# Attention then MLP on one core: a new issue order, 64-column transposes, loads of 96 and 48 rows, v in one load

## Chip, cores, metric

One core of a Trainium2 chip runs the program. The time is device microseconds (us) of one execution. Lower is better. Most executions agree within 0.3 per cent; where a run's state is "slow" (over 1.5 per cent above the fastest of its kernel) or its executions scatter, this is said and its time isn't compared.

Names in what follows: PE is the matmul engine (TensorE), DVE is VectorE, ACT is ScalarE, and POOL in profile lines is GpSimd. SBUF and PSUM are the on-chip memories; PE's results go to PSUM.

## What is computed

```python
def _attn_ref(q, k, v):              # B=8, H=8, S=576, D=64, float32
    scores = q @ k.T / sqrt(D)
    rel = pos[:, None] - pos[None, :]
    mask_plain = (rel >= 0) & (rel < 32)                       # heads 0..3
    mask_dil   = (rel >= 0) & (rel < 128) & (rel % 4 == 0)     # heads 4..7
    ...                                                        # softmax, then @ v
def _moe_ref(x, w_in, w_out):        # x: 4608 x 512; w_in: 512 x 2048; w_out: 2048 x 512
    h = x @ w_in
    return (h * sigmoid(h)) @ w_out
```

The MLP has nine groups of 512 tokens. A group needs 64 + 64 matmuls of 128x128 by 512 columns. Attention of a batch is many small matmuls.

## The kernel before

q and k of a batch are loaded in two pieces of 72 rows (a row here is four neighbouring positions of the sequence, all heads). Two heads at a time are transposed on PE into a PSUM tile, 8 transposes a tile, and copied to SBUF; for heads 0 to 3 ("first heads") by four ACT copies, since the two heads' halves come out on the wrong partitions. I call such a set of transposes a *tile*; a batch has eight (k and q, four pairs of heads each).

```python
ps_mm = tile_pool(name="ps_mm", bufs=3, PSUM)   # h and y of the MLP
ps_t  = tile_pool(name="ps_t",  bufs=1, PSUM)   # one transpose tile
...
def trans(nm, hp):
    tps = ps_t.tile([P, 2, 2, 2, MH], F16, ...)            # MH = 72
    for hi in range(2):
        for rp in range(2):
            for t in range(2):                             # the two loaded pieces
                nc.tensor.transpose(tps[:, hi, rp, t],
                    nats[nm, t][:, 2 * hp + hi, 2 * rp : 2 * rp + 2, :], ident[:MH, :MH])
    ...
    if hp >= HP // 2:                                      # heads 4..7: one DVE copy
        nc.vector.tensor_copy(dst, src); return
    for hi in range(2):                                    # heads 0..3: four ACT copies
        for ri in range(2):
            nc.scalar.copy(dst, src[rs, hi])
...
for step in attention(0): step()
for g in range(NG):                                        # MLP group g, attention g+1
    steps = mlp(g)                                         # 16 layer-1, then 16 layer-2 steps
    for i, step in enumerate(steps):
        step()
        # attention steps of batch g+1 dealt out evenly over the MLP steps
        upto = min(len(att), (i + 1) * len(att) // (len(steps) - 2))
        ...
```

The softmax here doesn't subtract the row's maximum and nothing guards it: scores larger than these inputs give would overflow.

## Time and profile before

419.46 us (median). What matters:

| part of the span | us |
|---|---|
| start-up, up to the first MLP matmul | 40.1 |
| seven groups, each with the next batch's attention | 44.6 to 46.3 each |
| two groups of MLP alone | 27.6 each |
| drain | 4.1 |

The windows view, cut where groups begin, shows this. Its columns are the stretch, its length, busy us (and number of instructions) of PE, PE's weight loads, DVE, ACT and GpSimd, then the granted clock of PE, the share of the DMA engines, and GB/s.

```profile
0.00:40.10 40.10, 15.60 (x204) 12.15 (x205) 18.02 (x69) 15.94 (x25) 25.56 (x51) 1.00 1.33 143
86.24:131.28 45.04, 40.02 (x334) 19.69 (x332) 25.92 (x68) 25.63 (x44) 9.22 (x12) 0.89 0.54 68
358.52:386.15 27.63, 27.63 (x129) 12.51 (x128) 11.01 (x16) 11.94 (x20) 0.00 (x0) 1.00 0.13 39
```

A mixed group takes 45.0 us, though neither DVE nor ACT is busy for more than 26 us of it, and an MLP group alone needs 27.6 us. The waits view (who waited for what: us in total, times, longest) and the page's row of granted clock (tenths of full speed, 40 slices) say why.

```profile
PE tq_0_1165 L164 <- ACT kP_1132 L182: 2.6, 1, 2.6
PE tq_1_1216 L164 <- ACT kP_1132 L182: 1.2, 1, 1.2
```

```profile
PEclk9999989986999699988998699969997799999999
```

PE waits for ACT's four copies at the head of each group, and after such gaps the clock is granted at half speed for a while (the 6s and 7s). The 1.00 of the first row isn't a reading: the trace's record of the clock begins at 49.3 us, and until then matmuls of 512 columns start 0.43 us apart instead of 0.216, as they do at a clock of 0.50. One more reading, which the prediction missed, stands in the timeline of the kernel before (start, duration, engine, line, tile and operands, partitions x columns).

```profile
56.19 1.03 PE L303 MATMUL h_6_684<-xT,w_in_88 128*128 128x512 f16 x4
57.15 0.30 PE L193 MATMUL s_1_692<-qP_551,kP_552 64*128 64x96 f16 x6
57.38 1.04 PE L303 MATMUL h_7_701<-xT,w_in_88 128*128 128x512 f16 x4
58.26 0.20 PE L164 MATMUL tq_2_709<-ident,q_nat_0_175 72*128 72x72 f16 x1
58.30 0.19 PE L164 MATMUL tq_2_709<-ident,q_nat_1_177 72*128 72x72 f16 x1
```

From start to start, h_7 takes 0.88 us when a 72-row transpose follows. The same work in h_6 takes 0.96 us when a 64-row score step follows. So about 0.1 us is lost at the step from 128 rows to 64. It is no single case: at full clock the last MLP matmul before a 72-row transpose takes 0.216 us from start to start (median of 35), before a 64-row score matmul with the same 72 columns of moving data 0.311 us (median of 21). Transposes of 72 rows among themselves go at 0.03 us each.

### The profile page before, as it was taken

What the parts mean: (1) busy time and instruction counts of PE and PEld (TensorE: products, weight loads), DVE (VectorE), ACT (ScalarE), POOL (GpSimd) and SP (SyncE); (2) the same over time, 40 slices, a digit from 0 to 9 for tenths busy, and PEclk for the clock granted to TensorE, in tenths of its full rate; (3) what the DMA queues carried; (4) which work ended last, traced back from release to release, by engine and by line L of the source; (5) the groups of instructions that cost most, each with busy time, mean ns of one, the idle gap of its engine ahead of it and who ended that gap; (6) DMA issues with size and microseconds to landing.
All of it is one profiled execution on the core that took longest, in us unless ns stands there. A gap on an engine that the chain in (4) does not pass through costs nothing.

```text
span 417.9 us, 7058 instructions
## 1 busy us (share of the span) xinstructions
PE 351.6 (84%) x2784; PEld 175.1 (42%) x2784; DVE 221.0 (53%) x578; ACT 218.8 (52%) x373; POOL 85.2 (20%) x128
## 2 busy tenths in 40 slices
PE   0266699978996799969997899779995999999996
PEld 0244344533453345424453345334542445444442
DVE  2077168524963377516952496328742685560730
ACT  2840975169614963197516861496319651451631
POOL 8933638200620035001610062000000000000000
PEclk9999989986999699988998699969997799999999
DMA  8999999910891029200991079100020002102102
GB/s 100 122 199 142 156 179 138 186 31 2 98 140 52 0 35 171 59 27 0 145 109 36 2 90 149 51 1 2 25 52 25 2 2 62 40 1 78 25 25 77
DMA packets 67746, 29.60 MB, mean 71 GB/s; under 512 B 34944, under 2 KB 63104, under 8 KB 67712
## 3 DMA queue, kind: packets, MB, share of 16 engines
q0 software_dynamic: 62080, 19.70, 46.2%
q1 hardware_dynamic: 5632, 9.44, 7.7%
q8 instruction: 22, 0.36, 0.4%
q14 instruction: 12, 0.10, 0.1%
HBM read 39.32 MB, written 9.44 MB: 117 GB/s over the span
## 4 chain that ended last, share of the span: by engine, by line
PE 68%; ACT 16%; DVE 11%; issue 3%; DMA 1%; POOL 0%; ACTq 0%; DVEq 0%; POOLq 0%
ACT kP_192 L182 2%; DMA k_nat_1_113<-in_k_dram 1%; ACT kP_2292 L182 1%; ACT kP_2873 L182 1%; ACT kP_1132 L182 1%; ACT kP_4025 L182 1%; ACT kP_3452 L182 1%; ACT kP_1713 L182 1%; ACT kP_552 L182 1%; PE y_0_1454 L321 1%; PE y_0_3195 L321 1%; PE y_0_2035 L321 1%; PE y_0_874 L321 1%; PE y_0_4347 L321 1%; PE y_0_3774 L321 1%
## 5 line engine op out<-in xcount | busy, mean ns | idle before, releaser
L303 PEld LDWEIGHTS <-w_in_88 128*128 128x128 f16 x576 | 53.4, 106 | 56.5 <-issue 14.9
L100 POOL DMA_DIRECT2D vp_104<-in_v_dram x24 | 18.0, 751 | 23.6 <-DMA w_in_88<-in_moe_w_in_dram 5.3
L100 POOL DMA_DIRECT2D vp_103<-in_v_dram x24 | 17.9, 754 | 18.2 <-DMA q_nat_0_1708<-in_q_dram 2.4
L224 DVE TENSOR_TENSOR probs_91<-probs_91,mask_p 128x576 f16<-128x576 f16 x3 | 1.4, 454 | 15.3 <-ACT probs_91 L222 15.3
L321 PEld LDWEIGHTS <-gT_4800 128*128 128x128 f16 x64 | 6.3, 98 | 7.5
L321 PEld LDWEIGHTS <-gT_4587 128*128 128x128 f16 x64 | 6.2, 97 | 7.6
L312 DVE SCALAR_TENSOR_TENSOR gT_4800<-th_0_4806,h_0_4801 128x512 f16<-128x512 f32 x1 | 0.7, 687 | 14.0 <-ACT th_0_4806 L311 14.0
L82 POOL DMA_DIRECT2D k_nat_0_2283<-in_k_dram x1 | 0.8, 848 | 31.0 <-PE tk_3_1897 L164 31.0
L82 POOL DMA_DIRECT2D k_nat_0_3443<-in_k_dram x1 | 0.8, 848 | 30.5 <-PE tk_3_3057 L164 30.5
L82 POOL DMA_DIRECT2D k_nat_0_2864<-in_k_dram x1 | 0.8, 848 | 30.3 <-PE tk_3_2476 L164 30.3
L321 PEld LDWEIGHTS <-gT_555 128*128 128x128 f16 x64 | 5.3, 97 | 4.1
L321 PEld LDWEIGHTS <-gT_3455 128*128 128x128 f16 x64 | 5.3, 97 | 4.1
L321 PEld LDWEIGHTS <-gT_2876 128*128 128x128 f16 x64 | 5.3, 97 | 4.1
L321 PEld LDWEIGHTS <-gT_4028 128*128 128x128 f16 x64 | 5.3, 97 | 4.1
L321 PEld LDWEIGHTS <-gT_2295 128*128 128x128 f16 x64 | 5.3, 97 | 4.1
L321 PEld LDWEIGHTS <-gT_1716 128*128 128x128 f16 x64 | 5.3, 97 | 4.1
L321 PEld LDWEIGHTS <-gT_1135 128*128 128x128 f16 x64 | 5.3, 97 | 4.1
L182 ACT COPY kP_192<-tk_0_195 64x288 f16<-64x288 f16 x4 | 3.2, 790 | 7.1 <-PE tk_0_195 L164 7.1
L94 POOL DMA_DIRECT2D vraw_107<-in_v_dram x8 | 5.9, 744 | 4.2 <-DMA w_out_89<-in_moe_w_out_dram 3.1
L311 ACT ACTIVATE th_0_561<-h_0_556 128x512 f32<-128x512 f32 x1 | 0.6, 597 | 11.5 <-PE h_0_556 L303 11.5
L94 POOL DMA_DIRECT2D vraw_108<-in_v_dram x8 | 5.9, 743 | 3.1 <-DMA w_in_88<-in_moe_w_in_dram 1.7
L82 POOL DMA_DIRECT2D k_nat_0_1704<-in_k_dram x1 | 0.8, 848 | 27.0 <-PE tk_3_1316 L164 27.0
(1845 smaller groups left out, 1117.3 us busy)
## 6 DMA issues: line engine op xcount, KB each, us to landing
w_in_88<-in_moe_w_in_dram POOLq DMA_DIRECT2D x4, 512.0 KB, 8.9
w_out_89<-in_moe_w_out_dram POOLq DMA_DIRECT2D x4, 512.0 KB, 9.7
vp_103<-in_v_dram POOLq DMA_DIRECT2D x24, 64.0 KB, 4.4
vp_104<-in_v_dram POOLq DMA_DIRECT2D x24, 64.0 KB, 7.0
vraw_107<-in_v_dram POOLq DMA_DIRECT2D x4, 208.0 KB, 9.2
vraw_108<-in_v_dram POOLq DMA_DIRECT2D x4, 208.0 KB, 9.9
vraw_107<-in_v_dram POOLq DMA_DIRECT2D x4, 144.0 KB, 9.8
vraw_108<-in_v_dram POOLq DMA_DIRECT2D x4, 144.0 KB, 9.5
```

The lines of the kernel that those rows point to most:

```text
L82: nc.gpsimd.dma_start(out=d.rearrange("p h r d -> p h (r d)"), in_=src[b].rearrange("h (m r) d -> m h (r d)", r=DIL)[t * MH : (t + 1) * MH],)
L94: nc.gpsimd.dma_start(out=vraw[p0 : p0 + n, ab].rearrange("p h r d -> p h (r d)"), in_=src[m0 : m0 + n],)
L100: nc.gpsimd.dma_start(out=vp[:, j, :, :D], in_=v[b, :HN, k0 : k0 + P, :].rearrange("h p d -> p h d"),)
L182: nc.scalar.copy(dst, src[rs, hi])
L224: nc.vector.tensor_tensor(pm, pm, mk, ALU.mult)
L303: nc.tensor.matmul(h, w_in16[:, c, f * P : (f + 1) * P], xT[:, c, t0 : t0 + GT], start=(c == 0), stop=(c == HP - 1),)
L311: nc.scalar.activation(th, h, AF.Tanh, scale=0.5)
L312: nc.vector.scalar_tensor_tensor(gT[:, f], th, 1.0, h, ALU.add, ALU.mult)
L321: nc.tensor.matmul(y, gT[:, f, tb * P : (tb + 1) * P], w_out16[:, f], start=(f == 0), stop=(f == NFF - 1),)
```

## The change

Its intent: keep PE fed. A small model of PE, ACT and DVE in the build picks the next step for PE from attention, layer 1 and layer 2, so that layer-2 matmuls fill the waits of attention. The first heads are transposed in 64-column pieces that land on the right partitions, so one ACT copy replaces four. The loads get row counts that are multiples of 16, in the hope that more DMA engines share them. v's six overlapping windows come in one load. The diff, cut to its core:

```diff
-    nat = ...(name="nat", bufs=8)
+    nat = ...(name="nat", bufs=4)
-    ps_mm = (bufs=3) ... ps_a = (bufs=2) ... ps_t = (bufs=1)
+    ps_h = (bufs=2); ps_y = (bufs=1); ps_x = (bufs=3)
...
+    TS = ((0, MA), (MA, M - MA))                       # MA = 96, M = 144
+        rest = nat.tile([P, H, DIL, D], F16, tag="rest", bufs=2)   # k's 48 rows at 0, q's at 64
+            first = nat.tile([MA, H, DIL, D], F16, tag="first", bufs=4)
...
-        for j in range(NB):
-            nc.gpsimd.dma_start(out=vp[:, j, :, :D], in_=v[b, :HN, k0 : k0 + P, :]...)
+        nc.gpsimd.dma_start(out=vp[:, j0:, :D], in_=win)     # all windows at once
...
+            if hp < HP // 2:                           # first heads
+                tps = small(ring, [P, DIL, M], F16, ...)
+                for r in range(DIL):
+                    for t, (m0, n) in enumerate(TS):   # 96 rows, then 48 rows
+                        for hi in range(2):
+                            nc.tensor.transpose(tps[hi * D : (hi + 1) * D, r, m0 : m0 + n],
+                                nats[nm, t][0][:, 2 * hp + hi, r, :], nats[nm, t][1])
+                yield "ACT", 0.56                      # what the model is told of the copy
+                nc.scalar.copy(...)                    # one copy, k or q
...
+            for hi in range(2):                        # heads 4..7, 128 columns as before
+                for rp in range(2):
+                    for t, (m0, n) in enumerate(TS):
...
+        for b, st, ring_of in att[:LOOK]:              # attention first, if it is ready
+        for q_, lim in ((l1, 1.3), (l2, 9.0)):         # then layer 1, then layer 2
```

It also makes the masks with less GpSimd work and copies batch 0's x on ACT.

## The prediction

> **What bounds the kernel now.** The windows view, cut at the group boundaries in the chain of waits: 0–40.1 us is start-up (PE busy 15.6 us); then seven groups of MLP matmuls interleaved with the next batch's attention take 44.6–46.3 us each; the last two groups, pure MLP with no PE gap, 27.6 us each; 4.1 us to drain. In a mixed group DVE is busy 25.9 us and ACT 25.5 us, so neither bounds it: PE does, badly fed.
>
> PE work that a mixed group needs at the fast clock: 27.6 us of MLP plus about 6.7 us of attention (spacings in the timeline: 8 transposes 0.26 us, a score step 0.24, an attention-times-V step 0.125, x transposes about 1.0 in all) = 34.3 us. So 10–12 us per group is lost. Two causes. First, PE waits at its head: the waits view has the q transposes waiting 2.6 us and 1.2 us for ACT's kP copies (4 × 0.79 us per tile, one PSUM buffer). Second, after these gaps matmuls are spaced 0.43 us instead of 0.216 from about 91 to 100 us; PEclk there is 0.51. The Trainium skill ("TensorE: Matmul & The Clock Gate", Part 1) says idleness halves the clock for windows of about 3.4 us; this trace agrees.
>
> **What the change does.**
> - The 64-column transposes land both heads' halves on the right partitions: 4 ACT copies of a tile (3.2 us for k, 1.6 for q) become one full-width copy, estimated 0.65 us like the 128x576 exp (0.645). ACT loses about 7 us per batch, and the 2.6 us waits go. Cost: 16 PE transposes instead of 8, about 0.5 us instead of 0.26, +1 us PE per batch (risk: narrow weight loads may be slower, up to 0.9 us).
> - The order fills attention's ACT/DVE latencies with layer-2 steps of the previous group, so the clock should stay up. Two h buffers allow one layer-1 step per about 1.2 us alone; they are interleaved. One y buffer costs about 0.8 us where y tiles follow directly, roughly 9 times, mostly in the tail.
> - Start-up: POOL's masks (5.3–10.5 us) shrink, so v and weights are issued sooner; 72-row loads become 96 and 48. The skill ("DMA: Bandwidth & Descriptors", how many engines) gives 12 engines for 72 rows and 16 for 96 or 48; the trace's DMA share of 0.82 in 0–10 us is compatible. Batch 0's x moves to ACT, spare PSUM is used. I expect attention(0) done at about 26 us instead of 40, but PE then reaches batch 1's transposes after two layer-1 steps and waits for those loads until about 33 us (before: landing 35–41).
>
> **Sum.** 33.5 us until batch 1's loads + remaining PE work 247 (MLP) + 7 × 7.6 (attention) = 300, + 6 for a cold clock and late w_out/v in the first group, + 7 for order mismatches, + 6 for y waits, + 4 drain ≈ 355; rounded down a little for overlap: **352 us**, range 338–370. Chances: faster 0.98, same 0.01, slower 0.01. All of it lies on PE's path: about 8 us per mixed group, 5–10 from the start.
>
> **What shows it.** Right: mixed groups 35–38 us, PE busy over 95% from 50 us on, PEclk near 1.00 after start-up, no PE wait on kP over 0.5 us, ACT busy down by about 55 us in total, first layer-1 matmul at 24–29 us. Wrong if: PEclk still drops to 0.5–0.8 between groups; 64-column transposes spaced over 45 ns; PE stalled over 3 us by v of batch 1 or w_out; the single-load v (3072 descriptors) holding POOL or landing late.
>
> **What would make it wrong.** In-order PE stalls because real latencies exceed the build-time ones, repeatedly re-triggering the slow clock; or slower start-up loads.

## The result

441.31 us (440.74 to 441.5) against 419.46 us. The ratio of the fast runs is 1.0523, 95 per cent interval 1.0496 to 1.055: slower by 5 per cent. Here and below a ratio is the mean time of one kernel's fast runs over that of the other's from the same rounds, so it's not quite the ratio of the medians quoted.

The page of the profile after, its rows of busy time and granted clock:

```profile
PE 410.1 (93%) x3040; PEld 204.9 (47%) x3040; DVE 217.0 (49%) x580; ACT 170.9 (39%) x287; POOL 52.7 (12%) x74
PEclk9999579959985997799769995999699999999999
```

What was intended did happen: ACT fell from 218.8 to 170.9 us, and no wait of PE for kP is left among the PE waits listed. But PE is busy for 410.1 us instead of 351.6, and the clock still falls, once per batch. The timeline of the changed kernel at the head of a batch, first a tile of 64 columns at full clock, then one of 128 columns at half clock:

```profile
124.08 0.23 PE L264 MATMUL tk_0_1601<-ident,k_first_709 96*64 96x96 f16 x2
124.24 0.21 PE L264 MATMUL tk_0_1601<-ident,rest_708 48*64 48x48 f16 x2
124.38 0.23 PE L264 MATMUL tk_0_1601<-ident,k_first_709 96*64 96x96 f16 x2
...
125.29 0.23 PE L264 MATMUL tq_0_1620<-ident,q_first_712 96*64 96x96 f16 x2
...
130.90 0.26 PE L282 MATMUL tk_2_1691<-ident,k_first_709 96*128 96x96 f16 x1
131.09 0.22 PE L282 MATMUL tk_2_1691<-ident,rest_708 48*128 48x48 f16 x1
131.24 0.26 PE L282 MATMUL tk_2_1691<-ident,k_first_709 96*128 96x96 f16 x1
```

A 64-column tile runs from 124.08 to 125.29, 1.21 us. In the kernel before a tile took 0.26 us. Even the 128-column tiles, which the change left alone but for the row counts, take 0.35 us per pair here, 1.4 us per tile; before, at half clock, they took about 0.5 us. What the windows view has for these stretches:

```profile
120.00:130.00 10.00, 10.00 (x98) 5.70 (x96) 4.02 (x9) 4.94 (x8) 0.00 (x0) 0.96 0.09 26
130.00:140.00 10.00, 10.00 (x54) 4.74 (x53) 3.76 (x8) 2.39 (x4) 2.25 (x4) 0.50 0.36 41
```

PE counts as busy for every one of these 20 us (a matmul counts until its modelled end), and the clock is at 0.50 in the second ten. So "busy" says nothing here about how fast PE gets on.

### The profile page after: what moved, and what is told of

The parts are those of the page before. It is cut to its first block, busy times and chain, and to the rows that moved or that the text cites. A ratio compares the mean times of both kernels' runs of the same rounds, so it can differ in the third digit from the quotient of the medians.

```text
span 439.7 us, 7382 instructions
## 1 busy us (share of the span) xinstructions
PE 410.1 (93%) x3040; PEld 204.9 (47%) x3040; DVE 217.0 (49%) x580; ACT 170.9 (39%) x287; POOL 52.7 (12%) x74
## 4 chain that ended last, share of the span: by engine, by line
PE 88%; DVE 5%; ACT 3%; DMA 2%; issue 1%; POOL 0%; ACTq 0%; POOLq 0%
DMA rest_114<-in_q_dram 2%; PE y_2_2752 L486 2%; PE y_2_3225 L486 1%; PE y_2_3867 L486 1%; PE y_2_2087 L486 1%; PE y_0_1589 L486 1%; PE y_1_1046 L486 1%; PE y_3_4877 L486 1%; PE y_1_4835 L486 1%; PE y_0_4814 L486 1%; PE y_3_4793 L486 1%; PE y_2_4772 L486 1%; PE y_2_4561 L486 1%; PE y_2_4856 L486 1%; PE y_3_3984 L486 1%; PE y_3_4581 L486 1%
## 5 line engine op out<-in xcount | busy, mean ns | idle before, releaser
L459 PEld LDWEIGHTS <-w_in_83 128*128 128x128 f16 x576 | 54.0, 100 | 61.7 <-issue 9.3
L486 PEld LDWEIGHTS <-gT_4598 128*128 128x128 f16 x64 | 6.2, 97 | 11.1 <-issue 4.0
L486 PEld LDWEIGHTS <-gT_4386 128*128 128x128 f16 x64 | 6.2, 98 | 9.3 <-issue 1.9
L486 PEld LDWEIGHTS <-gT_4048 128*128 128x128 f16 x64 | 6.2, 98 | 9.3 <-issue 1.9
L486 PEld LDWEIGHTS <-gT_1675 128*128 128x128 f16 x64 | 6.3, 107 | 7.9 <-issue 3.4
L103 POOL DMA_DIRECT2D vraw_103<-in_v_dram x8 | 5.4, 678 | 36.5 <-DVE vd_101 L334 34.5
L486 PEld LDWEIGHTS <-gT_3497 128*128 128x128 f16 x64 | 6.0, 98 | 7.8 <-issue 1.0
L486 PEld LDWEIGHTS <-gT_2380 128*128 128x128 f16 x64 | 6.2, 105 | 7.2 <-issue 2.2
L486 PEld LDWEIGHTS <-gT_2941 128*128 128x128 f16 x64 | 6.1, 104 | 7.2 <-issue 2.3
L486 PEld LDWEIGHTS <-gT_1197 128*128 128x128 f16 x64 | 6.1, 105 | 6.8 <-issue 2.2
L486 PEld LDWEIGHTS <-gT_558 128*128 128x128 f16 x64 | 5.8, 101 | 6.6 <-issue 1.7
L103 POOL DMA_DIRECT2D vraw_102<-in_v_dram x8 | 5.4, 678 | 21.5 <-DVE vd_100 L334 19.3
L264 PE MATMUL tk_0_208<-ident,k_first_115 96*64 96x96 f16 x8 | 1.2, 288 | 6.8 <-DMA k_first_115<-in_k_dram 6.8
L486 PE MATMUL y_2_2752<-w_out_84,gT_1675 128*128 128x512 f16 x16 | 6.9, 595 | 0.0
L299 PEld LDWEIGHTS <-kP_111 64*128 64x128 f16 x96 | 3.2, 111 | 7.6 <-issue 7.5
L316 PEld LDWEIGHTS <-kD_108 64*128 64x128 f16 x128 | 3.2, 102 | 7.1 <-issue 6.8
L486 PE MATMUL y_2_3225<-w_out_84,gT_2380 128*128 128x512 f16 x16 | 6.5, 567 | 0.0
L299 PEld LDWEIGHTS <-kP_110 64*128 64x128 f16 x96 | 3.2, 111 | 6.3 <-issue 5.9
L316 PEld LDWEIGHTS <-kD_109 64*128 64x128 f16 x128 | 2.9, 96 | 6.8 <-issue 6.8
L119 POOL DMA_DIRECT2D vp_99<-in_v_dram x4 | 5.7, 1430 | 2.1 <-DMA q_first_170<-in_q_dram 1.8
L486 PE MATMUL y_2_3867<-w_out_84,gT_2941 128*128 128x512 f16 x16 | 5.9, 523 | 0.0
L119 POOL DMA_DIRECT2D vp_98<-in_v_dram x4 | 5.8, 1444 | 0.8 <-PE tk_1_610 L264 0.6
```

The source lines that it names most:

```text
L103: nc.gpsimd.dma_start(out=vraw[p0 : p0 + m1 - m0, ab].rearrange("p h r d -> p h (r d)"), in_=src[m0:m1],)
L119: nc.gpsimd.dma_start(out=vp[:, j0:, :D], in_=win)
L264: nc.tensor.transpose(tps[hi * D : (hi + 1) * D, r, m0 : m0 + n], nats[nm, t][0][:, 2 * hp + hi, r, :], nats[nm, t][1],)
L299: nc.tensor.matmul(sp[:, i, QB * jj : QB * (jj + 1)], kP[r, hp, QB * j : QB * j + P], qP[r, hp, :, QM * j : QM * (j + 1)], start=True, sto ...
L316: nc.tensor.matmul(sp[:, i, c : c + MH], kD[r, h, rp, ab * KB : ab * KB + P], qD[r, h, rp, ab * MH : (ab + 1) * MH], start=True, stop=True,)
L459: nc.tensor.matmul(h, w_in16[:, c, f * P : (f + 1) * P], xT[:, c, t0 : t0 + GT], start=(c == 0), stop=(c == HP - 1),)
```

## Theories

- **A, row heights.** A transpose of 48 rows next to one of 96 rows can't overlap with it. The loads of 96 and 48 rows make PE alternate within each tile. In its narrower form, A2, only the step between at most 64 rows and more than 64 rows costs; in A1 any difference does.
- **B, column width.** The 64-column transposes are slow in themselves.
- **C, order.** The new order puts transposes in long runs, and the clock falls because of that.

A is also what the Trainium skill leads to ("TensorEngine Tiling (Array Packing)", Tiling Modes, Key Properties): "Changing tiling mode (not just tile) drains the TensorE", and it has separate modes for 128 and for 64 rows. I hadn't looked this up before predicting; I had thought of row counts as a matter of the DMA only.

## Experiments

Twelve kernels ran. All gave correct results. "e2" and the like are used as short names.

### e1_grouped: same transposes, other order inside a tile

```diff
-                for r in range(DIL):
-                    for t, (m0, n) in enumerate(TS):
+                for t, (m0, n) in enumerate(TS):
+                    for r in range(DIL):
                         for hi in range(2):
```
(and the same swap in the 128-column tiles)

> The changed kernel with the transposes of a tile reordered: all 96-row pieces first, then all 48-row pieces. Same instructions, loads and step order. Theory A (a transpose whose row height differs from the one before it cannot overlap its weight load, so each change of height costs about 0.1 us): a 64-column tile of 16 transposes falls from 1.21 us to under 0.7 us, a 128-column tile from 1.39 us to about 0.5 us, PE busy falls by 35 to 50 us, time 385 to 405 us. Theory B (64-column transposes are slow in themselves): the 64-column tiles stay near 1.2 us, only the 128-column ones get faster, time 410 to 425. Theory C (a run of transposes lets the clock fall whatever their speed): the phases at clock 0.5 stay about 10 to 14 us per batch.

Measured: **371.54 us**, ratio 0.8863 (0.8832 to 0.8894). Its rows of busy time and clock, and its timeline:

```profile
PE 339.9 (92%) x3040; PEld 171.9 (46%) x3040; DVE 215.4 (58%) x580; ACT 168.8 (46%) x287; POOL 52.7 (14%) x74
PEclk9999999999999989999999999999999999999999
```

```profile
132.36 0.36 PE L264 MATMUL tk<-ident,k_first 96*64 96x96 f16 x8
132.65 0.30 PE L264 MATMUL tk<-ident,rest 48*64 48x48 f16 x8
132.88 0.36 PE L264 MATMUL tq<-ident,q_first 96*64 96x96 f16 x8
133.18 0.30 PE L264 MATMUL tq<-ident,rest 48*64 48x48 f16 x8
133.41 0.30 PE L299 MATMUL s<-qP,kP 64*128 64x96 f16 x6
133.65 0.34 PE L282 MATMUL tk<-ident,k_first 96*128 96x96 f16 x4
133.92 0.27 PE L282 MATMUL tk<-ident,rest 48*128 48x48 f16 x4
134.12 0.34 PE L282 MATMUL tq<-ident,q_first 96*128 96x96 f16 x4
```

The same instructions in the same kernel, only swapped inside a tile: 64-column tiles went from 1.21 to 0.52 us (132.36 to 132.88), 128-column ones to 0.47 us, PE is busy 70 us less, and the clock holds but for one stretch of 3.4 us (the 8; mean 0.995). That is 70 us of time for two swapped loops, more than theory A had asked for (385 to 405 us). The order of steps on PE is that of the change, so C falls: runs of fast transposes all but leave the clock alone. B falls as to its main claim: the 64-column tiles got faster without getting wider.

### e2_rows72: all pieces of one height

```diff
-    TS = ((0, MA), (MA, M - MA))
+    TS = ((0, MH), (MH, MH))          # 72 and 72 rows, four tiles of their own
-    o32 = ...(bufs=3)
+    o32 = ...(bufs=2)                 # room for them
```

> The changed kernel with q and k loaded in two pieces of 72 rows as before, all of one height; everything else and the step order as in the change (output buffers 3 to 2 to make room, which should cost nothing). Theory A: 64-column tiles under 0.7 us, 128-column tiles 0.26 us warm as before, time 375 to 400 us; the q and k loads land 2 to 3 us later at the start. Theory B: 64-column tiles stay near 1.2 us, time 405 to 420.

Measured: **365.15 us**, ratio 0.8721 (0.8695 to 0.8748), below the 375 to 400 us that A gave. The timeline, at two places:

```profile
38.25 0.45 PE L262 MATMUL tq<-ident,q_nat 72*64 72x72 f16 x16 [0.29 <-ACT kP L269]
38.64 1.04 PE L457 MATMUL h<-xT,w_in 128*128 128x512 f16 x4
...
129.88 0.43 PE L262 MATMUL tk<-ident,k_nat 72*64 72x72 f16 x16
130.14 0.43 PE L262 MATMUL tq<-ident,q_nat 72*64 72x72 f16 x16
130.78 0.30 PE L297 MATMUL s<-qP,kP 64*128 64x96 f16 x6 [0.21 <-ACT qP L274]
131.02 0.43 PE L280 MATMUL tk<-ident,k_nat 72*128 72x72 f16 x8
131.32 0.42 PE L280 MATMUL tq<-ident,q_nat 72*128 72x72 f16 x8
```

Sixteen 64-column transposes start at 129.88 and the next tile at 130.14: 0.26 us, as long as eight 128-column ones took before. The two heads of a pair start 0.003 us apart, the pairs about 0.03 us. So inside a tile the 64-column form costs PE nothing when the heights are equal, where the prediction had put 0.5 us with a risk of 0.9. A change of width does cost: the tile at 38.25, with an MLP matmul next, takes 0.39 us. Into such a tile the last MLP matmul takes 0.309 us instead of 0.216 (6 cases), and out of it the last transpose 0.131 us instead of 0.032 (8 cases), as much as a step of height. This happens some 20 times in e2, about 2 us in all (an estimate). The skill's page on tiling ("TensorEngine Tiling (Array Packing)", Tile-to-Partition Mapping, Restrictions) says that column tiling disables fast weight loads; no cost of that shows here.

### e3_cols128: e2 with the transposes and the four ACT copies of before

```diff
-                nc.scalar.copy(...)                       # one copy
+                yield "ACT", 2.8 if nm == "k" else 1.2
+                for hi in range(2):
+                    for ri in range(2):
+                        nc.scalar.copy(dst, tps[rs, hi])  # 8 transposes of 128 columns before it
```

> As e2, but the first heads' tiles transposed 128 columns wide with four ACT copies each, as before; the build-time model is told 2.8 us (k) and 1.2 us (q) of ACT. So it is the changed issue order with the transposes and row heights of before. Theory A and a good order: 375 to 400 us, 128-column tiles 0.26 us warm, and the clock low for under 5 us per batch. If the order itself is what goes wrong (runs of transposes without MLP matmuls between), the clock phases stay at 10 us per batch and the time stays above 405.

Measured: 384.71 us, ratio 0.9191 (0.9144 to 0.9238). This is 19.6 us slower than e2: that is what the 64-column form with its single copy is worth inside the new order. In the waits view q's transposes wait 4.6 and 1.9 us for ACT's copies again, and scores 5.8 us for exps (0.7 us in e2), probably queued behind these copies. The mean clock was 0.988, so the order isn't what let the clock fall.

### e4_before9648: the kernel before, with loads of 96 and 48 rows alone

```diff
-                d = nat.tile([MH, H, DIL, D], ...)                   # 72 rows each
+                m0, n = ((0, 96), (96, 48))[t]
+                d = nat.tile([n, H, DIL, D], ...)
```

> The kernel before with only the loads changed to 96 and 48 rows (transposes alternate 96 and 48 rows). Theory A: each tile of 8 transposes goes from 0.26 us to about 1.0 us warm, so about 6 us more PE time per batch, partly hidden in waits: 425 to 460 us. Theory B: same time as before within 1 per cent, or a little faster from the start.

Measured: 467.54 us, ratio 1.1164 (1.1129 to 1.1199), above the range given. This one part of the change, put into the kernel before, costs 48 us. In its timeline the eight transposes take 1.09 us at full clock (121.22 to 122.31):

```profile
120.35 1.04 PE L304 MATMUL h<-xT,w_in 128*128 128x512 f16 x4
121.22 1.16 PE L165 MATMUL tk<-ident,k_nat 96*128 96x96 f16 x8
122.31 1.90 PE L304 MATMUL h<-xT,w_in 128*128 128x512 f16 x8
```

Here only 128-column transposes occur, so B had expected no loss. A is confirmed in a second kernel.

### e12_before_grouped: e4 with the two heights grouped

```diff
-            for hi in range(2):
-                for rp in range(2):
-                    for t in range(2):
+            for t in range(2):
+                for hi in range(2):
+                    for rp in range(2):
```

> e4 (the kernel before with loads of 96 and 48 rows, 1.116 of the kernel before) with the transposes of a tile reordered, the four 96-row ones first, then the four 48-row ones: one step of height per tile instead of seven. If the steps between heights are the whole fault, it comes back to within 2 per cent of the kernel before, 415 to 428 us; a small rest is expected, since one step inside each tile and one between tiles remain. If the shorter loads cost something else too, it stays above 435 us.

Measured: 428.5 us, ratio 1.0214 (1.0181 to 1.0247), just above the expected range. 39 of e4's 48 us come back by the reorder. About 9 us stay, with one step of height inside each tile and one from tile to tile. So the shorter loads were no gain in the kernel before in any form tried.

### e5_80_80 and e6_96_80: which difference of height matters

```diff
+    TS = ((0, 80), (M - 80, 80))      # e5: rows 0..80 and 64..144, overlap loaded twice
+    TS = ((0, 96), (M - 80, 80))      # e6: rows 0..96 and 64..144
```

> As e2, but two pieces of 80 rows each that overlap by 16 rows (rows 0 to 80 and 64 to 144; the overlap is loaded and transposed twice). One height everywhere and 11 per cent more bytes and columns. Theory A: 64-column tiles about 0.30 us and 128-column tiles about 0.29 us warm (80/72 of those of e2), time 360 to 368 us, within 1 per cent of e2; the last q piece of batch 0 lands about 1 us sooner than in e2 (13.0 us) if 72 rows use fewer DMA engines than 80.

> As e5, but pieces of 96 and 80 rows (rows 0 to 96 and 64 to 144), alternating within each tile as in the change. Both are over 64 rows. Theory A1 (any difference of height stops the overlap): tiles as slow as in the change, 1.2 us, time 430 to 460 us. Theory A2 (only the step between a piece of at most 64 rows and one of more than 64 rows does): tiles about 0.33 us, time 362 to 373 us.

Measured: e5 364.5 us, ratio 0.868 (0.8654 to 0.8706); e6 365.91 us, ratio 0.8715 (0.8692 to 0.8738). In e6 the heights alternate 96, 80, 96, 80 just as 96 and 48 do in the change. Its timeline:

```profile
130.50 0.50 PE L262 MATMUL tk<-ident,k_nat 96*64 96x96 f16 x16
130.83 0.50 PE L262 MATMUL tq<-ident,q_nat 96*64 96x96 f16 x16
```

0.33 us per tile. So A1 falls and A2 stands: it isn't the difference as such. 96 with 80 rows is free, 96 with 48 costs. In the transposes the columns moved change together with the rows (48 or 80). The kernel before separates them: after the same MLP matmul, 64 rows lose 0.1 us and 72 rows nothing, both with 72 columns moved. So it is the rows, and the boundary lies between 64 and 72, which fits the skill's modes. What one step costs, worked out: (1.21 - 0.26) / 8 = 0.12 us in a 64-column tile and (1.09 - 0.26) / 8 = 0.10 us in a 128-column one, near the 0.1 us seen before each score step in the kernel before.

e5 also tests the loads. PE's waits for the four pieces of batch 0 in e2 and in e5, from the timeline (the time in brackets is PE's wait before, and for what):

```profile
6.55 0.27 PE L262 MATMUL tk<-ident,k_nat 72*64 72x72 f16 x2 [6.55 <-DMA k_nat<-in_k_dram]
13.00 0.63 PE L262 MATMUL tq<-ident,q_nat 72*64 72x72 f16 x14 [1.81 <-DMA q_nat<-in_q_dram]
```

```profile
6.50 0.28 PE L262 MATMUL tk<-ident,k_nat 80*64 80x80 f16 x2 [6.50 <-DMA k_nat<-in_k_dram]
11.56 0.68 PE L262 MATMUL tq<-ident,q_nat 80*64 80x80 f16 x14 [1.38 <-DMA q_nat<-in_q_dram]
```

After the first piece, three of 72 rows take 6.45 us, three of 80 rows 5.06 us although they are longer. Per row that is 1.42 times faster. By the rule in the skill ("DMA: Bandwidth & Descriptors", How many engines), the largest divisor of the row count up to 16, 72 rows get 12 engines and 80 rows 16, an estimated factor of 1.33; the trace agrees roughly. The page also names an exception for some loads that GpSimd issues, as these are, so the engine counts themselves are not shown here. In the whole time it's worth at most half a per cent.

### e7_spread: slow transposes kept, never two tiles in a row

```diff
+            if b > 0 and st.is_t and last_t[0] and (l1 or l2):
+                waits.append(plan.t + 0.3)
+                continue
-                st = Step(None, 0.45, "ring", [at_qk], ...)
+                st = Step(None, 1.2, "ring", [at_qk], ...)
```

> The changed kernel, its slow alternating 96/48 transposes kept, but the step order never puts two of these tiles in a row while an MLP step is ready (the build-time model is told 1.2 us for a tile). If the low clock comes from long runs of slow transposes with a nearly idle array: the clock stays at 1.0 except at the start, PE still spends about 1.2 us per 64-column tile and about 1.0 us per 128-column tile, so about 45 us more PE time than e2: 395 to 420 us. If the low clock comes from anything else, it stays: 430 to 445 us.

Measured: 437.08 us in the median, but scattered from 426.44 to 447.55, and the profiled run was slow. No ratio is given, and the time is not compared. Only its clock is used, and the one fast run, 426.44 us, had a mean clock of 0.960 (e2: 0.998), so the clock fell there too. The page's clock row falls in most batches. The timeline just before the fall at 124.7 us, one MLP step, a tile, a score step, a tile, one MLP step:

```profile
120.31 1.04 PE L488 MATMUL y<-w_out,gT 128*128 128x512 f16 x4
121.28 0.23 PE L265 MATMUL tk<-ident,k_first 96*64 96x96 f16 x2
...
122.50 0.30 PE L300 MATMUL s<-qP,kP 64*128 64x96 f16 x6
122.73 0.23 PE L265 MATMUL tq<-ident,q_first 96*64 96x96 f16 x2
...
123.94 1.14 PE L488 MATMUL y<-w_out,gT 128*128 128x512 f16 x4
```

```profile
PEclk9999999859976997599957999999679999999999
```

My idea that *long* runs of slow transposes are needed for the clock to fall is refuted: two tiles with a short score step between them came before this fall. That a full MLP step between every two tiles wouldn't hold it is not shown, since the rule of this run lets a score step count as a break. What stays true in all runs: where tiles alternated over the boundary the clock fell in most batches (change, e4, e7); where the same tiles were fast in the new order it stayed up (e1, e2, e5, e6). e4 says little here, since in the kernel before the clock falls in each batch without any alternation, after waits. What exactly the clock's monitor counts stays open.

### e8_ytail: more buffers for y at the end

```diff
-                tiles[tb] = ps_y.tile([P, DM], F32, tag="y", ...)
+                pool, tag = (ps_x, "x") if g >= NG - 2 else (ps_y, "y")
+                tiles[tb] = pool.tile([P, DM], F32, tag=tag, ...)
```

> As e2, but the layer-2 results of the last two groups take turns in the three PSUM buffers that attention no longer uses, instead of the single one. In e2 PE waited 7.1 us in 12 waits of 0.7 us for the single buffer, 10 of them in the last two groups. Expected: 5 to 7 us less than e2, 358 to 361 us; if the waits come back elsewhere, 363 to 366 us.

Measured: 359.49 us, ratio 0.8558 (0.8531 to 0.8585). The waits of PE for the single y buffer, in e2 and then in e8:

```profile
PE y L484 <- ACT ob L495: 7.2, 12, 0.7
```

```profile
PE y L485 <- ACT ob L496: 2.9, 6, 0.7
```

4.3 us of waits went, and about 5.7 us of time (the two runs come from different rounds).

### e9_best, e10_static, e11_v6: both gains together, and two parts undone

e9 is e5 with e8's buffers. e10 is e9 with the order of before (attention dealt out evenly over the MLP steps). e11 is e9 with v in six loads.

```diff
-    while att or l1 or l2: ...                       # e10: no model
+    for g in range(NG): ...                          # MLP steps, attention g+1 dealt out evenly
-        nc.gpsimd.dma_start(out=vp[:, j0:, :D], in_=win)          # e11
+        for j in range(NB): nc.gpsimd.dma_start(out=vp[... j ...], in_=win)
```

> e5 (80 and 80 rows) and e8 (y of the last two groups in the three idle buffers) together. Each alone gave 0.868 and 0.856 of the kernel before, e2 0.872. If they add up: 357 to 360 us, 0.850 to 0.858 of the kernel before.

> e9 with the issue order of the kernel before in place of the one from the build-time model: batch 0's attention, then each group's MLP steps with the next batch's attention steps dealt out evenly among them. Loads, transposes, copies and buffers are those of e9. If the order is worth much: 375 to 395 us, with waits at layer 1 (two h buffers, no layer-2 step between) and the clock at times low. If the cheaper tiles did the work and not the order: 358 to 368 us.

> e9 with v's sliding windows in six loads a batch (seven for batch 0), as before, instead of one. If v in one load matters only to GpSimd's issue time, which is off the chain: within 1 per cent of e9, 356 to 363 us, GpSimd busy up by about 25 us. If it matters at the start, where loads are issued in a row: 2 to 4 us slower.

Measured: e9 **358.97 us**, ratio 0.8567 (0.8551 to 0.8583); e9 and e8 agree within 0.2 per cent, so e5's gain doesn't show on top of e8's. e10 382.37 us, ratio 0.9134 (0.9109 to 0.9158): with e9's buffers, which were laid out for the new order, the order is worth 23.4 us. Its largest waits, beside those for the first loads, are those the order was made to avoid:

```profile
PE y L485 <- ACT ob L496: 11.5, 21, 0.6
PE h L457 <- DVE gT L468: 10.4, 27, 0.5
```

In e9 these are 2.9 us and 1.7 us. The clock is no part of it: e10's mean was 0.995. e11 358.8 us, ratio 0.8561 (0.8545 to 0.8576): the same as e9. GpSimd is busy 77.9 instead of 53.3 us, and it doesn't matter, as it isn't on the chain.

## Why the prediction was wrong, point by point

- **The direction.** 352 us, faster, was predicted; 441 us, slower, was measured. The step that failed is the term "7 × 7.6 (attention)" in the sum, and in it "16 PE transposes instead of 8, about 0.5 us instead of 0.26, +1 us PE per batch". Measured at full clock: 1.21 us per 64-column tile (change), and 1.09 us per 128-column tile (e4), for which no extra was budgeted at all. For 64 tiles in the whole run that is 32 × (1.21 - 0.26) + 32 × (1.09 - 0.26) = 57 us, an estimate from those durations. The change is 76.8 us longer than e2 in the profiled spans (439.7 and 362.9). The rest of about 20 us is put down to the lower clock (0.899 against 0.998); this split is worked out, not measured by a run of its own, as e7 failed to hold the clock. Of the signs that the prediction named for being wrong, two came: 64-column transposes spaced over 45 ns (1.21 us / 16 = 76 ns) and a clock that still drops. But so did one that it named for being right, PE busy over 95 per cent from 50 us on (375.5 of 389.7 us, 96 per cent).
- **The reason.** Row counts were weighed only as a matter of DMA engines. That they also set the height of every transpose on PE wasn't considered. The named risk, "narrow weight loads may be slower", pointed at the wrong cause: at equal heights narrow transposes cost nothing inside a tile (e2).
- **"The clock should stay up"**: wrong for the change, right without the fault (0.995 to 1.000 in e1, e2, e5, e6).
- **ACT's loss and the kP waits.** About 55 us less ACT work was predicted, 48 us measured; the kP waits went. Right.
- **The order.** Its gain was predicted as about 8 us per mixed group together with the copies. e10 and e3 show 23 us for the order and 20 us for the transposes with one copy. Together they would be 6 us per group (43 / 7), if the two pairs of runs may be added. Directly, from the first MLP matmul to the last, e2 takes 325.3 us and the kernel before 373.7, 6.9 us per group: near it.
- **Start-up.** The first MLP matmul was predicted at 24 to 29 us; it came at 37.8 us, and at 33.4 us without the fault (e2). The prediction was too early in either case; why was not tested. PE ran cold until 37 us in e2 (its MLP matmuls from 33.4 us on start 0.43 us apart), with waits for ACT and DVE. In the sum the error counts less, since batch 1's transposes were expected from 33.5 us and began at 37.0 us in e2.
- **y waits.** About 6 us in the tail predicted, 7.2 us in 12 waits measured (e2). Right.
- **v in one load** held GpSimd for about 1.4 us per load, and no wait of PE for it is listed. The fear of it was unfounded (e11).

With the alternation removed, e2 and e1 land at 365 and 372 us; e2 is inside the range given, e1 just outside. The rest of the sum was about right; one mis-sized term of it was enough to turn the sign.

## What to carry to other kernels

Before you choose how many rows a piece has for the DMA's sake, look at what runs on PE with that piece: keep neighbouring matmuls on one side of the boundary of 64 rows and of one width, or group them, since each crossing cost about 0.1 us here, three to four times the 0.03 us between 128-column transposes. Such crossings remain in every kernel here: each of the 64 score steps has 64 rows and can be entered and left across the boundary, up to 64 x 2 x 0.1 = 13 us, an estimate; no run tried to remove them. When PE is busy nearly all the time and the kernel still got slower, measure start-to-start times of the same work before and after; the busy share hides instructions that no longer overlap. A large change that loses may hold good parts: here swapping two loops turned 5 per cent slower into 11 per cent faster, and equal heights with a few more buffers made it 14 per cent faster than the kernel before.

## What the Trainium skill lacked or had wrong

- "TensorEngine Tiling (Array Packing)": it says that a change of mode drains the engine, but gives no cost. Measured: 0.10 to 0.12 us per step between 96 and 48 rows; none visible between 96 and 80 rows (0.33 us for 16 transposes); about 0.1 us also per step between 128-column matmuls and 64-column transposes of 72 rows (0.309 instead of 0.216 us, e2).
- The same page says column tiling disables fast weight loads. No penalty shows inside a tile: 16 transposes of 64 columns took 0.26 us, the same as 8 of 128 columns.
- "TensorE: Matmul & The Clock Gate": it tells of the clock falling after idle windows. Here it fell to 0.50 in a stretch in which the profile has PE busy for 10.00 of 10.00 us, and in the kernel before it fell at 90.2 us after a window of 3.4 us that was not idle: PE was busy for 1.44 us of it. The page's Part 4 says of the transpose mode that it doesn't count as PE-busy in the same way, but gives no measure; the same transposes left the clock at 0.995 when grouped by height (e1). What is counted stays open.
- "DMA: Bandwidth & Descriptors", How many engines: the rule roughly agrees, though it leaves open which loads its exception covers; 80-row pieces came 1.42 times faster per row than 72-row ones, where 16 against 12 engines gives an estimated 1.33.
- No page connects the row count of a load with the row mode of the matmuls that use it, which was the trap here.
